# Separate PSUM tiles for the second feed-forward matmul and for the transposes of q and k in a fused retention and feed-forward kernel

## The chip, the cores and the metric

The kernel runs on one core of one Trainium2 chip. The metric is the device time of one execution in microseconds (us). The kernel before takes 328.62 us (median of 3 runs, 328.57 to 328.68). Profiles are of one execution each, and their span is about 2 us shorter than the timed run.

## The reference

Retention with a decay per head, then a feed-forward block with the activation h·cos(h):

```python
# q, k, v: (8 batches, 8 heads, 576 positions, 64), w_in: (512, 2048), w_out: (2048, 512), float32
scores = (1 / np.sqrt(64)) * np.matmul(q, k.transpose(0, 1, 3, 2))
gamma = 1.0 - 2.0 ** (-5.0 - np.arange(H))
Dmat = np.where(rel >= 0, gamma[:, None, None] ** rel[None], 0.0)      # rel = pos_i - pos_j
attn = np.matmul(scores * Dmat, v)
x = attn.transpose(0, 2, 1, 3).reshape(4608, 512)
h = x @ w_in
out = (h * np.cos(h)) @ w_out
```

## The kernel before

The 4608 tokens are handled in 36 groups of 128 (retention) and in 10 chunks (feed-forward) of 512, 256, 256 and then seven times 512 tokens; they are numbered n = 0 to 9 here. A group needs q and k loaded, scaled in bf16 on POOL (`prep`), transposed (on TensorE for groups 0 to 7, by DMA afterwards), and multiplied. A chunk goes through `mm1` (first matmul, sine on ACT, product on DVE) and `mm2` (second matmul in blocks of 128 tokens, each 16 accumulating matmuls of 512 columns, then an eviction by ACT and a DMA out). While `mm2` of one chunk runs, the retention of later groups is slipped in between its matmuls at fixed places.

All PSUM tiles come from one pool with one buffer per tag. Counted in banks, here units of 512 fp32 columns on each partition, the tags a, b and m are two banks wide (an `mm1` block of 1024 fp32 columns), st and n one bank each: the kernel uses eight. A new tile on a tag waits until everything that used the tag's previous tile is done. A write into one part of a tile, in the kernel before, waits for the reader of the tile's other part too, as the trace shows below.

The parts that change:

```python
    def transposes(g, early=False):
        qks, vb, qkT = tiles["a", g]
        # ... groups from 8 on: DMA transpose, and return
        ps = psum.tile([P, 2, 2 * HG, P], BF16, tag="b" if early or g % 2 else "a", name="tr")
        for m in range(2):                                   # m = 0: q, m = 1: k
            for hg in range(HG):
                nc.tensor.transpose(ps[:, m, hg, :],
                    qks[:, m, 2 * hg : 2 * hg + 2, :].rearrange("s h d -> s (h d)"), ident)
            nc.scalar.copy(qkT[:, m * HG : (m + 1) * HG, :], ps[:, m, :HG, :])

    def mm2(n, tsi, et):
        gT = tiles["g", n]
        wide = tsi in (1, 2) if n != 2 else tsi == 0
        if et == 0:
            if not wide:
                tiles["o"] = psum.tile([P, DM], F32, tag="n", name="o")
            elif tsi < 2:
                tiles["oo"] = psum.tile([P, 2, DM], F32, tag="m", name="oo")
        ps = tiles["oo"][:, tsi // 2, :] if wide else tiles["o"]
        nc.tensor.matmul(ps, lhsT=gT[:, et, tsi * P : (tsi + 1) * P],
                         rhs=w_out_sb[:, et, :], start=(et == 0), stop=(et == ET - 1))
        if et == ET - 1:
            ot = op.tile([P, DM], F32, tag="o", name="ot")
            nc.scalar.copy(ot, ps)                           # the eviction
            # ... DMA out, feed(s)

    for g in range(4):                                       # the start
        # ... for g == 3: the weight loads, load(4, gate=w_dma[1]), load(5)
        transposes(g, early=True)
        nc.scalar.copy(tiles["a", g][1], tiles.pop(("fv", g)))
        scores(g, "a")
        if g < 3:
            prep(g + 1, early=True)
        state(g)
        if g < 3:
            attn_out([g], "m")

    # chunk n takes these tags, one per mm1 block:
    banks = {0: "bambambam", 1: "mbam", 2: "bmab", 3: "mamabmab"}.get(n, "bmabmabm")
```

So the four blocks of a 512-token chunk went to n, first half of m, second half of m, n.

## Time and profile before

| quantity | value | view |
|---|---|---|
| time | 328.62 us | timed runs |
| TensorE (PE) busy | 92% | page, part 1 |
| PE in the chain that ended last | 89% | page, part 4 |
| `mm2` waiting for its own eviction | 4.7 us in 7 waits | waits view |
| transposes waiting for ACT's copies | 5.7 us in 8 waits | waits view |

The page of the kernel before, parts 1 and 4 (engine shares):

```profile
PE 299.6 (92%) x2208; PEld 168.8 (52%) x2240; DVE 175.1 (54%) x177; ACT 115.6 (35%) x132; POOL 99.4 (30%) x122
PE 89%; ACT 4%; DVE 2%; issue 2%; DMA 1%; POOL 0%; DVEq 0%; POOLq 0%
```

PE is the bottleneck, so time is won where PE stands still. The waits view says what PE waited for (us in total, times, longest us):

```profile
PE tr L141 <- ACT qkT L146: 5.7, 8, 0.9
PE oo L269 <- ACT ot L278: 4.7, 7, 0.7
PE sc L154 <- ACT qkT L146: 2.7, 4, 0.7
```

The timeline of the last chunk shows one such wait (start us, duration us, engine, line, operation, out<-in, shapes, count, and in brackets the idle time before and its releaser):

```profile
308.31 3.62 PE L269 MATMUL o<-w_out_sb,gT 128*128 128x512 bf16 x16
311.76 3.62 PE L269 MATMUL oo<-w_out_sb,gT 128*128 128x512 bf16 x15
315.41 0.59 ACT L278 COPY ot<-oo 128x512 f32<-128x512 f32 x1 [2.87 <-PE oo L269]
316.05 3.61 PE L269 MATMUL oo<-w_out_sb,gT 128*128 128x512 bf16 x16 [0.67 <-ACT ot L278]
```

A block that is followed without a wait starts 3.45 us before the next one (308.31 to 311.76). The first half of oo starts 4.29 us before the second half. The difference, 0.84 us, is what a wait costs. The profile names only 0.67 us of it, because it counts from the modelled end of the last matmul, which lies about 0.17 us after the point at which the next one could have started. The Trainium skill ("TensorE: Matmul & The Clock Gate", Back-to-back issue gap) gives 512/2.4 + 2.5, about 216 ns, as the gap of a matmul taken by itself; here 3.45 us for 16 in a stream is the same 216 ns each.

A reader who knows the skill's page "Perfetto Trace Analysis" (Optimization Strategy) will recognise the pattern: it says that the same gap repeating on the engine that should be saturated can mean that there isn't enough memory for the next tile, and names buffer count and tile sizes. Here there was enough: the two halves of oo are 512 fp32 each, one bank each. What they shared was the tile.

The timeline at the transposes of groups 4 and 5, inside `mm2` of chunk 0, on PE:

```profile
46.67 0.39 PE L141 MATMUL tr<-ident,qks 128*128 128x128 bf16 x4
47.73 0.38 PE L141 MATMUL tr<-ident,qks 128*128 128x128 bf16 x4 [0.67 <-ACT qkT L146]
49.24 0.39 PE L141 MATMUL tr<-ident,qks 128*128 128x128 bf16 x4
50.57 0.38 PE L141 MATMUL tr<-ident,qks 128*128 128x128 bf16 x4 [0.94 <-ACT qkT L146]
50.79 1.24 PE L269 MATMUL oo<-w_out_sb,gT 128*128 128x512 bf16 x4
```

Four transposes hold PE for 0.22 us (50.57 to 50.79), but k's four start 1.06 us after q's four (46.67 to 47.73), because they write the other half of the tile that ACT is still reading. In groups 6 and 7, in the `mm2` of chunk 1, it is the same:

```profile
67.89 0.38 PE L141 MATMUL tr<-ident,qks 128*128 128x128 bf16 x4 [0.50 <-DVE gT L258]
68.94 0.38 PE L141 MATMUL tr<-ident,qks 128*128 128x128 bf16 x4 [0.67 <-ACT qkT L146]
70.46 0.39 PE L141 MATMUL tr<-ident,qks 128*128 128x128 bf16 x4
71.52 0.38 PE L141 MATMUL tr<-ident,qks 128*128 128x128 bf16 x4 [0.67 <-ACT qkT L146]
```

And the start, where group 3 hands over to the first `mm1` block:

```profile
22.96 0.61 PE L154 MATMUL sc<-qkT 64*128 64x128 bf16 x8 [0.68 <-ACT qkT L146]
23.90 3.62 PE L249 MATMUL h<-xT,w_in_sb 128*128 128x256 bf16 x16
```

### The profile page before, as it was taken

The numbers are of one execution on the slowest core, as the hardware profiler recorded it, in microseconds if no ns is written. First come the engines' busy times: TensorE is split into PE (matmuls) and PEld (weight loads), VectorE is DVE, ScalarE is ACT, GpSimd is POOL, SyncE is SP. The second block draws the span as 40 slices with busy tenths as digits, with TensorE's granted clock in tenths as the row PEclk, the third lists the DMA queues.
The fourth block names the chain that finished last, engine by engine and source line by source line (L and its number), as shares of the span: only waits on it lengthen the run. The fifth ranks groups of instructions, "written<-read, shape, count | busy, mean of one in ns | idle before, by whom it ended". The sixth has DMA issues, their size and how long they took to land.

```text
span 326.7 us, 5413 instructions
## 1 busy us (share of the span) xinstructions
PE 299.6 (92%) x2208; PEld 168.8 (52%) x2240; DVE 175.1 (54%) x177; ACT 115.6 (35%) x132; POOL 99.4 (30%) x122
## 2 busy tenths in 40 slices
PE   1669998979999989998999899989998999899995
PEld 1447844746768745444544454445444544454442
DVE  2644624345686755475547554765476546654600
ACT  4253632351515510551065105510551056105611
POOL 3670066662363635430633053305430000000000
PEclk9999999999999999999999999999999999999999
DMA  9999999999999999955992599259932610010011
GB/s 171 214 156 195 213 228 245 218 230 177 167 225 217 235 227 256 184 91 130 245 227 44 127 241 236 42 121 241 228 57 65 115 49 0 34 64 34 0 64 64
DMA packets 151512, 49.63 MB, mean 152 GB/s; under 512 B 142784, under 2 KB 146880, under 8 KB 151488
## 3 DMA queue, kind: packets, MB, share of 16 engines
q1 hardware_dynamic: 147264, 45.10, 72.9%
q0 software_dynamic: 4224, 4.19, 8.0%
q8 instruction: 17, 0.28, 0.4%
q14 instruction: 7, 0.06, 0.1%
HBM read 36.70 MB, written 9.44 MB: 141 GB/s over the span
## 4 chain that ended last, share of the span: by engine, by line
PE 89%; ACT 4%; DVE 2%; issue 2%; DMA 1%; POOL 0%; DVEq 0%; POOLq 0%
PE h L249 38%; PE oo L269 20%; PE o L269 19%; PE sc L154 3%; PE ov L224 3%; PE st L182 2%; ACT qkT L146 2%; PE tr L141 2%; PE ov L211 2%; ACT ot L278 2%; DVE ret L163 2%; DMA fq<-in_q_dram 1%; ACT cosh L257 1%; DVE gT L258 0%; POOL qks L124 0%
## 5 line engine op out<-in xcount | busy, mean ns | idle before, releaser
L249 PE MATMUL h<-xT,w_in_sb 128*128 128x256 bf16 (+1 forms) x762 | 128.6, 329 | 0.6 <-DVE ret L163 0.2
L258 DVE TENSOR_TENSOR gT<-h,cosh 128x1024 bf16<-128x1024 f32 x72 | 88.2, 1225 | 64.2 <-ACT cosh L257 64.0
L249 PEld LDWEIGHTS <-w_in_sb 128*128 128x128 bf16 x768 | 75.8, 99 | 51.9 <-issue 1.0
L257 ACT ACTIVATE cosh<-h,half_pi 128x1024 f32<-128x1024 f32 x72 | 80.2, 1113 | 54.8 <-PE h L249 54.8
L269 PEld LDWEIGHTS <-gT 128*128 128x128 bf16 x576 | 52.4, 98 | 62.2 <-issue 6.7
L124 POOL TENSOR_TENSOR qks<-fq,gq 128x512 bf16<-128x512 f32 x36 | 37.5, 1042 | 127.9 <-DMA fq<-in_q_dram 120.4
L269 PE MATMUL oo<-w_out_sb,gT 128*128 128x512 bf16 x278 | 68.5, 379 | 5.7 <-ACT ot L278 4.7
L269 PE MATMUL o<-w_out_sb,gT 128*128 128x512 bf16 x272 | 67.6, 379 | 1.6 <-issue 1.1
L163 DVE TENSOR_TENSOR ret<-sc,tri 128x1024 bf16<-128x1024 f32 x32 | 38.0, 1220 | 18.0 <-PE sc L154 18.0
L125 POOL TENSOR_TENSOR qks<-fk,gk 128x512 bf16<-128x512 f32 x34 | 35.4, 1042 | 6.7 <-DMA fk<-in_k_dram 5.2
L236 DVE CAST xT<-ov 128x1024 bf16<-128x1024 f32 (+1 forms) x20 | 22.3, 1116 | 25.7 <-PE ov L224 25.4
L278 ACT COPY ot<-oo 128x512 f32<-128x512 f32 x18 | 10.5, 586 | 71.1 <-PE oo L269 66.3
L191 DVE TENSOR_TENSOR sb<-st,diag_99 128x512 bf16<-128x512 f32 x32 | 21.9, 683 | 22.1 <-PE st L182 22.1
L278 ACT COPY ot<-o 128x512 f32<-128x512 f32 x18 | 10.5, 585 | 62.7 <-PE o L269 62.7
L131 POOL CAST vb<-fv 128x512 bf16<-128x512 f32 x32 | 19.5, 610 | 5.3 <-DMA fv<-in_v_dram 3.9
L141 PE MATMUL tr<-ident,qks 128*128 128x128 bf16 x64 | 7.8, 261 | 11.4 <-ACT qkT L146 5.7
L146 ACT COPY qkT<-tr 128x512 bf16<-128x512 bf16 x16 | 9.4, 586 | 18.6 <-PE tr L141 18.6
L154 PE MATMUL sc<-qkT 64*128 64x128 bf16 x288 | 12.4, 227 | 2.7 <-ACT qkT L146 2.7
L224 PE MATMUL ov<-ret,vb 128*64 128x128 bf16 x288 | 12.8, 232 | 1.6 <-DVE ret L163 1.6
L154 PEld LDWEIGHTS <-qkT 64*128 64x128 bf16 x288 | 8.5, 98 | 10.6 <-issue 5.9
L182 PEld LDWEIGHTS <-qks 128*128 128x128 bf16 (+1 forms) x128 | 9.6, 102 | 7.8 <-issue 2.5
L182 PE MATMUL st<-vb,qks 128*128 128x128 bf16 (+1 forms) x128 | 13.3, 230 | 0.0
(31 smaller groups left out, 56.0 us busy)
## 6 DMA issues: line engine op xcount, KB each, us to landing
out_dram<-ot SPq DMA_DIRECT2D x36, 256.0 KB, 3.7
fq<-in_q_dram SPq DMA_DIRECT2D x32, 256.0 KB, 4.3
fk<-in_k_dram SPq DMA_DIRECT2D x32, 256.0 KB, 4.7
fv<-in_v_dram SPq DMA_DIRECT2D x32, 256.0 KB, 4.8
w_in_sb<-in_moe_w_in_dram POOLq DMA_DIRECT2D x4, 512.0 KB, 8.5
w_out_sb<-in_moe_w_out_dram POOLq DMA_DIRECT2D x4, 512.0 KB, 16.3
fq<-in_q_dram SPq DMA_DIRECT2D x8, 128.0 KB, 4.8
fk<-in_k_dram SPq DMA_DIRECT2D x8, 128.0 KB, 5.1
```

Of the source, the lines that this page charges most:

```text
L124: nc.gpsimd.tensor_tensor(out=qks[:, 0], in0=fq, in1=tq, op=ALU.mult)
L125: (nc.vector if early and g in (0, 3) else nc.gpsimd).tensor_tensor(out=qks[:, 1], in0=fk, in1=tk, op=ALU.mult)
L154: nc.tensor.matmul(ps[:, he, hg, :], lhsT=qkT[d0 : d0 + D, HG + hg, :], rhs=qkT[d0 : d0 + D, hg, :], start=True, stop=True,)
L163: nc.vector.tensor_tensor(out=ret.rearrange("p a b i -> p (a b) i"), in0=ps.rearrange("p a b i -> p (a b) i"), in1=mask.unsqueeze(1).to_br ...
L182: nc.tensor.matmul(ps[:, hg, :], lhsT=qks[p0:, 1, 2 * hg : 2 * hg + 2, :].rearrange("s h d -> s (h d)"), rhs=vb[p0:, 2 * hg : 2 * hg + 2, ...
L224: nc.tensor.matmul(ps[he * D : he * D + D, x, hg, :], lhsT=vb[:, 2 * hg + he, :], rhs=ret[:, he, hg, :], start=(g % PER == 0 and hg == 0), ...
L236: nc.vector.tensor_copy(tiles["x", n][:, :, t0 : t0 + len(gs) * P].rearrange("p c (x i) -> p x c i", i=P), ps)
L249: nc.tensor.matmul(ps[:, j, :], lhsT=w_in_sb[:, dg, (et + j) * P : (et + j + 1) * P], rhs=xT[:, dg, c0 : c0 + w], start=(dg == 0), stop=(d ...
L257: nc.scalar.activation(cosh, ps, ACTF.Sin, bias=half_pi, scale=1.0)
L258: nc.vector.tensor_mul(gT[:, et : et + m, c0 : c0 + w], ps, cosh)
L269: nc.tensor.matmul(ps, lhsT=gT[:, et, tsi * P : (tsi + 1) * P], rhs=w_out_sb[:, et, :], start=(et == 0), stop=(et == ET - 1),)
L278: nc.scalar.copy(ot, ps)
```

## The change

The intent is to take these waits away without another bank: `mm2` alternates over two separate tiles (n, m, n, m), q and k are transposed into a tile each, and in the first four groups the q transpose of the next group goes ahead of the output matmuls of this one. No instruction is added or removed.

```diff
-    def transposes(g, early=False):
+    def transposes(g, banks=None, only=(0, 1)):
@@
-        ps = psum.tile([P, 2, 2 * HG, P], BF16, tag="b" if early or g % 2 else "a", name="tr")
-        for m in range(2):
+        for m in only:
+            ps = psum.tile([P, HG, P], BF16, tag=banks[m], name="tr")
             for hg in range(HG):
                 nc.tensor.transpose(
-                    ps[:, m, hg, :],
+                    ps[:, hg, :],
@@
-            nc.scalar.copy(qkT[:, m * HG : (m + 1) * HG, :], ps[:, m, :HG, :])
+            nc.scalar.copy(qkT[:, m * HG : (m + 1) * HG, :], ps)
@@ mm2
-        wide = tsi in (1, 2) if n != 2 else tsi == 0
         if et == 0:
-            if not wide:
-                tiles["o"] = psum.tile([P, DM], F32, tag="n", name="o")
-            elif tsi < 2:
-                tiles["oo"] = psum.tile([P, 2, DM], F32, tag="m", name="oo")
-        ps = tiles["oo"][:, tsi // 2, :] if wide else tiles["o"]
+            bank = "mn"[tsi % 2] if n == 2 else "nm"[tsi % 2]
+            tiles["o"] = psum.tile([P, DM], F32, tag=bank, name="o")
+        ps = tiles["o"]
@@ the start
-        transposes(g, early=True)
+        if g == 0:
+            transposes(g, "bn", only=(0,))
+        transposes(g, "bn", only=(1,))
@@
         if g < 3:
+            transposes(g + 1, "bn", only=(0,))
             attn_out([g], "m")
@@ groups 4 to 7
-        return [(place, lambda: transposes(g)), (place + 6, lambda: transposes(g + 1))]
+        return [
+            (place, lambda: transposes(g, "ab")),
+            (place + 6, lambda: transposes(g + 1, "ab")),
+        ]
```

## The prediction

> **What bounds the kernel now.** TensorE. The page gives PE 92% busy, the chain of waits is 89% PE, and the granted clock stays at 9 tenths or more. Idle time of PE in that chain can be won; the waits view names it: the second matmul's tile "oo" waits for its eviction by ACT 7 times (4.7 us of modelled idle time), transposes wait for ACT's copies 8 times (5.7 us).
>
> **What the change does.** No instruction is added or removed; only tiles and order change.
>
> 1. *Second matmul, chunks of 512 tokens (n = 3 to 9).* Before, blocks 1 and 2 are two halves of one tile, and block 2 starts only after block 1's eviction. In the last chunk (timeline) block 1 starts at 311.76 us and block 2 at 316.05, 4.29 us later. The Trainium skill ("TensorE: Matmul & The Clock Gate", Back-to-back issue gap) gives 512/2.4 + 2.5 = about 216 ns per matmul; the trace agrees: 308.31 to 311.76 is 16 matmuls, 216 ns each. So block 2 could start at 315.2, and the wait costs 0.84 us (ACT copy 0.59, the rest pipeline drain). With alternating tiles the order is n, m, n, m: each tile has 3.5 us to be evicted. Seven times 0.84 = 5.9 us off.
>
> 2. *A new wait.* Block 3 of the first chunk now lies in m, and the second chunk's first matmul block also takes m: it waits one eviction, +0.84 us. Later chunks start with another tile (or, after the 256-wide chunk, end on n), and their m block comes at least 8 matmuls (1.7 us) later: no wait.
>
> 3. *Transposes of groups 6 and 7.* q and k halves no longer wait for each other: today the transposes of k start 1.05 us after those of q, though four take 0.22. Two times 0.83 = 1.7 us off.
>
> 4. *Start (groups 0 to 3) and groups 4, 5.* Today a group takes 5.05 us. With the q transposes ahead, about 1.25 us leaves each turn; then loads and POOL's scaling (q1 ready at 8.7, q2 at 12.3, q3 at 15.9) begin to matter. I expect the scores of group 3 at about 19 us instead of 22.96. But the first h matmul needs the first part of w_in: issued at 15.86, fastest landing 5.6 us, so about 21.5 to 22 instead of 23.9. About 2 us gained. The transposes of groups 4 and 5 then lose their waits too (0.83 and 1.1 us), but k of group 5 leaves POOL at 48.2 us whatever PE does (DMA-bound). So the mm2 stream resumes at 48.5 instead of 50.79: 2.3 us gained in all up to there, rather than 4.
>
> **Sum:** -5.9 + 0.84 - 1.7 - 2.3 = -9.1 us, nearly all on the critical path, as PE is the chain. Predicted 319.6 us (2.8% faster), 8 in 10 between 318.2 and 321.3. Faster by over 2%: 0.92; within 2%: 0.07; slower: 0.01.
>
> **What would show it.** Waits of the second matmul for the ot copy vanish; one new wait of h for ot near 58 us, about 0.7 us; transposes of group 5 wait for POOL about 1 us; h starts at 21.5 to 22, waiting for the w_in DMA; each chunk from n = 3 on is 0.84 us shorter.
>
> **What would make it wrong.** Earlier work collides on the DMA queues (over 90% busy until 139 us) and delays group 5 or the weights; weights land later than I read; a PE clock that warms earlier or later at the start.

## The result

The changed kernel takes 319.69 us (median of 4 runs, 319.60 to 319.76), against 328.65 us before in the same rounds. The ratio is 0.9727 (95% interval 0.971 to 0.9744): 2.7% faster. Ratios here are the mean time of one kernel's runs over that of the other's of the same rounds, so not quite the ratio of the medians that are quoted.

The page of the changed kernel, parts 1 and 4:

```profile
PE 297.4 (94%) x2208; PEld 167.5 (53%) x2240; DVE 175.2 (55%) x177; ACT 115.6 (36%) x132; POOL 99.7 (31%) x122
PE 81%; DMA 8%; SPq 5%; POOL 2%; issue 2%; DVE 1%; ACT 1%
```

PE is still the bottleneck, but the chain has a new beginning: until 48 us it now runs through DMA, the load queue (SPq) and POOL. Its longest piece is the landing of a part of w_out (19.89 to 34.60 us), which the loads of groups 4 and 5 are made to wait for (`gate`); no run moved this gate. What stands in the waits view for PE, of the waits that matter here:

```profile
PE sc L154 <- ACT qkT L146: 2.7, 4, 0.7
PE h L249 <- DMA w_in_sb<-in_moe_w_in_dram: 1.5, 1, 1.5
PE tr L141 <- POOL qks L125: 0.8, 1, 0.8
PE h L249 <- ACT ot L275: 0.7, 1, 0.7
```

The waits of `mm2` for its eviction and of the transposes for ACT are gone; one wait of h for the eviction is new. The last chunk is one unbroken stream, from the timeline:

```profile
299.99 13.98 PE L266 MATMUL o<-w_out_sb,gT 128*128 128x512 bf16 x63
```

The transposes of groups 4 and 5, the first `mm1` block of chunk 1, and the transposes of groups 6 and 7, on PE:

```profile
44.02 0.72 PE L141 MATMUL tr<-ident,qks 128*128 128x128 bf16 x8
44.58 1.46 PE L266 MATMUL o<-w_out_sb,gT 128*128 128x512 bf16 x6
46.89 0.40 PE L141 MATMUL tr<-ident,qks 128*128 128x128 bf16 x4 [0.86 <-POOL qks L124]
48.07 0.40 PE L141 MATMUL tr<-ident,qks 128*128 128x128 bf16 x4 [0.78 <-POOL qks L125]
48.30 1.24 PE L266 MATMUL o<-w_out_sb,gT 128*128 128x512 bf16 x4
...
58.38 7.15 PE L249 MATMUL h<-xT,w_in_sb 128*128 128x256 bf16 x64 [0.67 <-ACT ot L275]
66.24 0.61 PE L141 MATMUL tr<-ident,qks 128*128 128x128 bf16 x8 [0.72 <-DVE gT L258]
...
67.98 0.61 PE L141 MATMUL tr<-ident,qks 128*128 128x128 bf16 x8
```

The eight transposes of groups 4, 6 and 7 now run as one piece each. Group 5's no longer wait for ACT, but for POOL, which scales that group's q and k almost back to back:

```profile
45.79 1.04 POOL L124 TENSOR_TENSOR qks<-fq,gq 128x512 bf16<-128x512 f32 x1 [0.35 <-DMA fq<-in_q_dram]
46.97 1.04 POOL L125 TENSOR_TENSOR qks<-fk,gk 128x512 bf16<-128x512 f32 x1
```

And the start:

```profile
19.14 0.40 PE L154 MATMUL sc<-qkT 64*128 64x128 bf16 x8 [0.68 <-ACT qkT L146]
21.58 3.12 PE L249 MATMUL h<-xT,w_in_sb 128*128 128x256 bf16 x16 [1.54 <-DMA w_in_sb<-in_moe_w_in_dram]
```

The scores of group 3 come 3.8 us earlier, the first h only 2.3 us earlier: it waits for the first part of w_in.

Where the time went can be followed by laying the same event of both timelines side by side. The last column is the growth of the lead from row to row. Single profiles scatter: in the seven profiles here of kernels that transpose these groups in separate tiles and leave the loads as they were, `mm2` resumes between 48.20 and 48.55 us.

| event (start on PE) | before, us | after, us | lead, us | growth |
|---|---|---|---|---|
| first h of chunk 0 | 23.90 | 21.58 | 2.32 | 2.32 |
| `mm2` resumes after group 5's transposes | 50.79 | 48.30 | 2.49 | 0.17 |
| first h of chunk 1 | 60.02 | 58.38 | 1.64 | -0.85 |
| first h of chunk 2 | 79.44 | 76.13 | 3.31 | 1.67 |
| first h of chunk 3 | 96.00 | 92.68 | 3.32 | 0.01 |
| first h of chunk 4 | 130.84 | 126.68 | 4.16 | 0.84 |
| first h of chunk 5 | 163.30 | 158.32 | 4.98 | 0.82 |
| first h of chunk 6 | 196.32 | 190.50 | 5.82 | 0.84 |
| first h of chunk 7 | 228.78 | 222.13 | 6.65 | 0.83 |
| first h of chunk 8 | 261.80 | 254.32 | 7.48 | 0.83 |
| first h of chunk 9 | 294.49 | 286.17 | 8.32 | 0.84 |
| end of the span | 326.7 | 317.5 | 9.2 | 0.9 |

### The profile page after: what moved, and what is told of

Read it like the earlier page. It is cut to its first block, busy times and chain, and to the rows that moved or that the text cites. A ratio compares the mean times of both kernels' runs of the same rounds, so it can differ in the third digit from the quotient of the medians.

```text
span 317.5 us, 5415 instructions
## 1 busy us (share of the span) xinstructions
PE 297.4 (94%) x2208; PEld 167.5 (53%) x2240; DVE 175.2 (55%) x177; ACT 115.6 (36%) x132; POOL 99.7 (31%) x122
## 4 chain that ended last, share of the span: by engine, by line
PE 81%; DMA 8%; SPq 5%; POOL 2%; issue 2%; DVE 1%; ACT 1%
PE o L266 37%; PE h L249 34%; SPq L101 5%; DMA w_out_sb<-in_moe_w_out_dram 5%; PE ov L224 3%; PE sc L154 3%; PE st L182 2%; PE ov L211 2%; DMA fk<-in_k_dram 2%; DMA fq<-in_q_dram 2%; POOL w_in_sb L328 1%; PE tr L141 0%; DVE ret L163 0%; DVE gT L258 0%; ACT ot L275 0%
## 5 line engine op out<-in xcount | busy, mean ns | idle before, releaser
L266 PE MATMUL o<-w_out_sb,gT 128*128 128x512 bf16 x550 | 132.7, 379 | 2.5 <-issue 1.8
L275 ACT COPY ot<-o 128x512 f32<-128x512 f32 x36 | 21.1, 586 | 127.7 <-PE o L266 123.5
L211 PEld LDWEIGHTS <-sb 128*128 128x128 bf16 x128 | 8.9, 103 | 3.7
L141 PEld LDWEIGHTS <-qks 128*128 128x128 bf16 x64 | 4.9, 115 | 10.9 <-POOL qks L124 7.3
```

## The experiments

Four kernels ran on the first chip (before: 328.27 us), four on the second (before: 328.64 us), four on the third (before: 328.33 us). The same kernel's median moved by up to 0.4 us from chip to chip, so terms below a microsecond are read from the traces. The 95% intervals of the ratios are at most 0.0017 to either side (0.0025 for the transposes alone). With its threshold of 2%, the record calls the two halves "same" and the kernel with groups 4 to 7 shared "unclear"; all three are nevertheless faster than before by more than the noise. All twelve gave correct results.

### Only the second matmul's tiles

```diff
 (the kernel before, with only this)
-        wide = tsi in (1, 2) if n != 2 else tsi == 0
-        ... tiles "o" on n and "oo" on m
+        bank = "mn"[tsi % 2] if n == 2 else "nm"[tsi % 2]
+        tiles["o"] = psum.tile([P, DM], F32, tag=bank, name="o")
```

> The kernel before with only the second matmul's alternation over two tiles. If the terms of the prediction are additive: 7 waits of 0.84 us go, one new wait of 0.84 us comes before the first h block of the second chunk, so 328.65 - 5.9 + 0.84 = about 323.6 us; the second matmul's stream after the transposes of group 5 resumes at 50.8 us as before. Rival: the start of the kernel carries most of the gain and the tiles of the second matmul little: then above 326 us.

Measured: 323.75 us (323.62 to 323.89), ratio 0.9861. The span fell from 326.7 to 321.5 us, 5.2 us, where 5.06 was expected. `mm2` resumed after the transposes at 50.65 us, as before, and h of chunk 1 waited 0.67 us for the eviction. The rival, that the tiles matter little, falls.

### Only the transposes

```diff
 (the changed kernel, with the second matmul's tiles put back)
-        bank = "mn"[tsi % 2] if n == 2 else "nm"[tsi % 2]
-        tiles["o"] = psum.tile([P, DM], F32, tag=bank, name="o")
+        wide = tsi in (1, 2) if n != 2 else tsi == 0
+        ... tiles "o" on n and "oo" on m
```

> The changed kernel with the second matmul put back on its old tiles. Additive: only the start (2.5 us by 48.3 us) and the transposes of groups 6 and 7 (1.7 us) are gained, so 328.65 - 4.2 = about 324.5 us, the seven waits of the oo matmuls for the eviction are back, and the wait of h for the eviction near 58 us is gone. Together with the run of the other half the two gains should add up to the whole change's 9.0 us within 0.3. Rival: the halves interact, and the sum differs by over 1 us.

Measured: 324.51 us (three runs within 0.10 us, one at 326.04), ratio 0.9894. The span is 322.5 us, 4.2 us less than before, as expected. The waits view has the seven waits back, and no wait of h for the eviction:

```profile
PE oo L269 <- ACT ot L278: 4.7, 7, 0.7
```

The two halves save 5.2 and 4.2 us of span, 9.4 together; the whole change saves 9.2. Read from these single profiles, they add up within 0.3 us, as expected. The medians don't resolve this: the halves save 4.5 and 3.8 us, 8.3 together, against 9.0 for the whole change in its own rounds and 8.3 in its repetition on the third chip (below). So no interaction shows that the scatter, some 0.7 us between these figures, would let one see.

### Without the q transpose ahead

```diff
-        if g == 0:
-            transposes(g, "bn", only=(0,))
-        transposes(g, "bn", only=(1,))
+        transposes(g, "bn")
@@
-            transposes(g + 1, "bn", only=(0,))
```

> The changed kernel without the q transpose ahead in groups 0 to 3 (the separate bank tiles stay). Theory: moving q ahead is off the critical path, because h then waits for w_in until about 21.6 us and the stream after group 5's transposes for POOL until 48.3 us. The scores of group 3 should come at about 20.4 us instead of 19.1, h still at 21.6, the time 319.7 us within 0.3. Rival: the groups' chain at the start sets the time, and about 1.2 us is lost: 320.9 us.

Measured: 319.98 us (319.82 to 320.26), ratio 0.9746. That was 0.3 us above the changed kernel, but on another chip, so both ran again:

> The changed kernel once more, as the reference on the same chip for the three runs that follow: 319.7 us within 0.3.

> The kernel without the q transpose ahead, once more, since the first try (319.98 us) left open whether 0.3 us is real. Theory (off the critical path): within 0.2 us of the changed kernel of this call. Rival (a small part lies on the path): 0.3 us or more slower in every round.

Measured: the changed kernel 320.04 us (319.57 to 320.17, ratio 0.9748), without q ahead 319.82 us (319.71 to 320.21, ratio 0.9744). There is no difference that the scatter would let one see. The trace of the first try shows why, on PE:

```profile
20.17 0.61 PE L154 MATMUL sc<-qkT 64*128 64x128 bf16 x8 [0.74 <-ACT qkT L146]
...
21.51 3.60 PE L249 MATMUL h<-xT,w_in_sb 128*128 128x256 bf16 x16 [0.20 <-DMA w_in_sb<-in_moe_w_in_dram]
...
48.45 1.24 PE L266 MATMUL o<-w_out_sb,gT 128*128 128x512 bf16 x4
```

The scores of group 3 are 1.0 us later than with q ahead, and it costs nothing: h starts at the same time, because it waits for w_in, only shorter (0.20 instead of 1.54 us). The part of the change that reorders instructions is off the critical path, though not by much: in this kernel the groups finish only 0.2 us before w_in lands. The separate tiles alone bring a group down from 5.05 to 4.27 us (scores at 11.62, 15.89 and 20.17), moving q ahead to about 3.9. What the start as a whole is worth can be read from two other runs: the kernel with only the second matmul's tiles and the one with groups 4 to 7 shared (below) differ in the start alone. `mm2` resumes at 50.65 and 48.69 us there, and the spans are 321.5 and 319.6 us: about 1.9 us.

The repetition of the changed kernel also shows a caution about the waits view. In it PE's transposes of group 5 are put down to ACT (0.66 us for "ACT ot"), while the weight load just ahead of them is put down to POOL; POOL ended that scaling at 46.88 us, ACT its copy at 46.90 us, and the transposes began at 46.94 us. Two releasers ended within 0.02 us, and the view names the later one.

### The first chunk starts on m

```diff
-            bank = "mn"[tsi % 2] if n == 2 else "nm"[tsi % 2]
+            bank = "mn"[tsi % 2] if n in (0, 2) else "nm"[tsi % 2]
```

> The changed kernel with the first chunk's second matmul starting on tile m and ending on n, so that the second chunk's first h block finds m free. Theory: the new wait costs one eviction[...], so 0.84 us is gained: 318.85 us, and the wait of h for the eviction copy near 58 us is gone. Rival: the h block would then wait for something else at that place (its input xT), and little is gained: within 0.3 us of 319.7.

Measured: 318.96 us (318.80 to 319.08), ratio 0.9714. The new wait is gone from the trace:

```profile
48.55 1.24 PE L266 MATMUL o<-w_out_sb,gT 128*128 128x512 bf16 x4
...
57.78 4.42 PE L249 MATMUL h<-xT,w_in_sb 128*128 128x256 bf16 x39
```

From the resumption to h it takes 9.23 us (57.78 - 48.55), against 10.08 us in the changed kernel (58.38 - 48.30): 0.85 us less. This letter in one string is a small mistake in the change, and its repair costs nothing.

### q and k loads of groups 4 and 5 ahead of their v loads

```diff
-            load(4, gate=w_dma[1])
-            load(5)
+            load(4, gate=w_dma[1], names="qk")
+            load(5, names="qk")
+            load(4, names="v")
+            load(5, names="v")
@@ (and the scalings on POOL in the same order)
```

> The changed kernel with the q and k loads (and their scaling) of groups 4 and 5 ahead of the v loads of both. Theory: the second matmul's stream stops before the transposes of group 5 because k of group 5 lands at about 46.9 us; one 256 KB load earlier in the queue is about 1.2 us, so the stream resumes at about 47.1 instead of 48.3 and the time is about 318.5 us (318.0 to 319.0). The waits of the transposes for POOL shrink from 1.6 us to about 0.8 or less. Rival: another thing (copies on ACT, v of group 4) takes the place of that wait, and the time stays within 0.3 us of 319.7.

Measured: 319.35 us (318.43 to 319.46), ratio 0.9715. The time missed the expected range (318.0 to 319.0). `mm2` resumed at 47.85 us, earlier than 48.30 but not at 47.1. In this execution POOL did the four scalings from 43.02 to 47.56 us, without a wait for a load from 44.52 us on. PE itself reached the transposes of group 5 only at 47.14 us and then waited 0.2 us for POOL. The gate of these loads, a landed part of w_out, also fell 0.8 us later than in the changed kernel's profile (the loads began at 35.41 instead of 34.62 us), and `mm2` had a wait of 0.35 us for w_out. Which of these delays counted most was not separated. Seen alone on its chip, 0.3 us could not be told from the scatter.

### Groups 4 to 7 in a shared tile again

```diff
-            (place, lambda: transposes(g, "ab")),
-            (place + 6, lambda: transposes(g + 1, "ab")),
+            (place, lambda: transposes_shared(g)),        # the old form: one tile, two halves
+            (place + 6, lambda: transposes_shared(g + 1)),
```

> The changed kernel with q and k of groups 4 to 7 transposed into one shared tile again, as before. Theory: groups 6 and 7 lose 0.83 us each; for groups 4 and 5 the lost time lies under the wait for POOL at 48 us and costs nothing: 319.7 + 1.7 = about 321.4 us, resumption still at 48.3 to 48.6 us. Rival: all four cost 0.83 us: 323.0 us.

Measured: 321.73 us (321.50 to 321.93), ratio 0.9793. `mm2` resumed at 48.69 us, 0.4 us later than in the changed kernel's profile, and in groups 6 and 7 k's transposes again started 1.05 us after q's, where 0.22 would do: 2 x 0.83 us. Together 2.1 us, which is the difference of the spans (319.6 and 317.5 us). Group 5, on PE:

```profile
47.39 0.40 PE L153 MATMUL tr<-ident,qks 128*128 128x128 bf16 x4
48.46 0.39 PE L153 MATMUL tr<-ident,qks 128*128 128x128 bf16 x4 [0.67 <-ACT qkT L158]
48.69 1.24 PE L278 MATMUL o<-w_out_sb,gT 128*128 128x512 bf16 x5
```

So of the four waits, the two of groups 4 and 5 cost 0.4 us together and not 1.7 (0.1 to 0.5 us, given the scatter of the resumption): they lie mostly under the wait for POOL. The rival, 323.0 us, falls.

### Every block on one tile

```diff
-            bank = "mn"[tsi % 2] if n == 2 else "nm"[tsi % 2]
+            bank = "n"
```

> The changed kernel with every block of the second matmul on the one tile n, so that each block waits for the eviction of the one before it. Theory: 0.84 us for each of three boundaries in seven chunks of 512 tokens (17.6 us), one to two more in the first chunk and one in each 256-wide chunk, less the wait of h for m, which goes; a few hidden tenths where state matmuls lie at the boundary: about 337 us (335 to 339). Rival: the waits partly hide behind each other or behind the attention work, and the cost is under 12 us.

Measured: 337.62 us (337.25 to 338.01), ratio 1.0277. That is 17.9 us more than the changed kernel. The waits view and the last chunk:

```profile
PE o L266 <- ACT ot L275: 15.6, 25, 0.7
...
319.71 3.61 PE L266 MATMUL o<-w_out_sb,gT 128*128 128x512 bf16 x16 [0.67 <-ACT ot L275]
324.00 3.61 PE L266 MATMUL o<-w_out_sb,gT 128*128 128x512 bf16 x16 [0.67 <-ACT ot L275]
328.28 3.61 PE L266 MATMUL o<-w_out_sb,gT 128*128 128x512 bf16 x16 [0.67 <-ACT ot L275]
```

(The first line is from the waits view, the others from the timeline.) The blocks are 4.28 and 4.29 us apart instead of 3.45. The 25 waits are three in each of the seven 512-token chunks, two in the first chunk and one in each 256-wide chunk. From the first h of one chunk to that of the next, a 512-token chunk now takes 2.1 to 2.5 us more than in the changed kernel, a 256-wide chunk 0.84 us more; the first chunk costs nothing net, since the new wait of h went. So the price of one boundary is 0.84 us where nothing else fills it; at the third boundary of most chunks retention work fills a part (the wait named there is 0.35 to 0.45 us).

### Both repairs together, and k of group 5 on DVE

The first kernel joins the tile order of the first chunk and the load order. The second adds, at place 31 of chunk 0's `mm2`:

```diff
-        nc.gpsimd.tensor_tensor(out=qks[:, 1], in0=fk, in1=tk, op=ALU.mult)       # group 5, POOL
+        nc.vector.tensor_tensor(out=qks[:, 1], in0=fk, in1=tk, op=ALU.mult)       # group 5, DVE
```

> The changed kernel with both repairs: the first chunk's second matmul starting on m, and the q and k loads of groups 4 and 5 ahead of their v loads. If the two waits are independent the gains add: 319.7 - 0.84 - 1.2 = about 317.6 us (317.0 to 318.2). Rival: the earlier stream only runs into the next wait (m not free, v of group 4 late), and one of the gains is lost: above 318.3 us.

> Both repairs once more, beside the changed kernel on the same chip: 0.84 us for the first chunk's tile order and 0.5 to 0.7 us for the load order (the trace of the first try showed the stream resuming at 47.6 instead of 48.3 us): 1.3 to 1.5 us faster than the changed kernel of this call.

> Both repairs, and k of group 5 scaled on DVE (0.69 us) instead of POOL (1.04 us). If the landing of k of group 5 at about 46.2 us and its scaling are what holds the stream, it resumes 0.3 us earlier, at about 47.3 us, and the time is 0.3 us below that of both repairs. Rival: DVE gets to it late, or the transposes then wait for ACT: no gain.

Measured: both repairs 318.39 us (317.94 to 319.37), ratio 0.9695, and 318.51 us (317.91 to 318.76), ratio 0.9699. On the third chip (the second of these two) that is 1.5 us less than the changed kernel beside it (320.04 us), as the second expectation had it; the first expectation, 317.6 us, was too good by 0.8 us, and the measured 318.39 us fell where its rival had been put (above 318.3). The part that came short is the load order: `mm2` resumed at 47.60 us in the first and 47.39 in the second, 0.7 and 0.9 us earlier than in the changed kernel's 48.30 and not 1.2. Here, other than with the load order alone, POOL stood waiting for k of group 5 to land (from the timeline of the first):

```profile
46.27 1.04 POOL L127 TENSOR_TENSOR qks<-fk,gk 128x512 bf16<-128x512 f32 x1 [0.63 <-DMA fk<-in_k_dram]
```

With k of group 5 on DVE: 317.78 us (317.74 to 318.08), ratio 0.9682, 0.7 us less than both repairs by the medians, but the ranges of the two overlap, and the traces show `mm2` resuming at 47.39 and 47.37 us, where 0.3 us between them was expected. The median moved the way the theory said; that the scaling on DVE is what moved it is not shown. DVE began the scaling as soon as k had landed:

```profile
46.39 0.69 DVE L128 TENSOR_TENSOR qks<-fk,gk 128x512 bf16<-128x512 f32 x1 [5.00 <-DMA fk<-in_k_dram]
```

The landing of k of group 5 is then what its scaling waits for, as it was with both repairs. This last version has the lowest median of all: 3.2% below the kernel before.

## Why the prediction was right

The prediction said 319.6 us (318.2 to 321.3), and 319.69 us was measured. Each term of its sum held:

- **Seven waits of the second matmul, 5.9 us.** Held. From chunk 3 on the lead grows by 0.82 to 0.84 us per 512-token chunk. The half of the change alone (5.2 us of span) and the kernel with one tile (17.9 us for 25 waits, some of them partly filled) show that it is the reuse of the tile that costs this.
- **A new wait of 0.84 us ahead of chunk 1.** Held: the lead falls by 0.85 us there, and giving the tile order of the first chunk the other letter wins 0.85 us back.
- **Transposes of groups 6 and 7, 1.7 us.** Held: the lead grows by 1.67 us, and the shared tile brings back 2 x 0.83 us.
- **The start and groups 4 and 5, 2.3 us.** Held, at 2.49 us in these two profiles. The scores of group 3 came at 19.14 us (19 was said), h at 21.58 (21.5 to 22), `mm2` resumed at 48.30 (48.5). The important half of this step was to stop adding: PE saves 3.8 us up to group 3's scores, of which h keeps 2.3 because w_in lands at 21.5 us, and what the transposes of groups 4 and 5 lose in waits is taken up by the wait for POOL. That wait also levels what lies between: chunk 0's `mm2` began 2.83 us earlier (38.23 against 41.06), and 2.49 us were left after it.
- **The reason given for that wait was half right.** The prediction calls k of group 5 "DMA-bound". In the changed kernel's profile q of group 5 waits for its load (0.35 us), and then POOL scales q and k almost back to back (45.79 and 46.97 us, 1.04 us each). It is load and POOL together, and moving the loads forward alone brought 0.45 us at the resumption of the expected 1.2 us. The transposes of group 5 waited 0.86 and 0.78 us for POOL, 1.6 us in all, where the prediction said about 1.
- **What the prediction did not say:** the q transpose ahead, a third of the change by its description, is worth nothing here. It follows from the prediction's own numbers (scores at 19 us, w_in at 21.5), and the kernel without it shows it. The prediction also put the whole 1.25 us that leaves each group down to q going ahead; about 0.8 of it comes from the separate tiles (5.05 to 4.27 us). The sum was safe from this slip because w_in, and then load and POOL, set the time up to there.

## What to carry to other kernels

In this kernel a PSUM tile with two halves was one tile to the waits: the second half's first matmul waited until the first half was evicted, though each half is a bank of its own. Measure one such wait by how much farther apart the starts of successive blocks lie (4.29 instead of 3.45 us, so 0.84 us), not by the idle time that the profile names (0.67 us), and count the boundaries that nothing fills. When alternating over tiles that other phases use too, check who takes each tile next: the order in one chunk decided whether 0.84 us was lost. And before adding up gains at the start, look for the first thing that PE cannot hasten (weights landing, loads and scaling of the next groups): gains ahead of it count only up to there.

## What the Trainium skill lacked or had wrong

- "TensorE: Matmul & The Clock Gate", Back-to-back issue gap: it says that a stream of weight load and matmul pairs sustains about 131 ns per matmul of 512 columns, and that the formula 512/2.4 + 2.5 over-counts there. Here a stream of exactly such pairs runs at 216 ns each (16 in 3.45 us, before and after), so the formula holds and the lower figure does not appear.
- The same page, PE-mode transpose, gives about 275 ns for a transpose in a kernel's context. The durations in this trace are like that (216 to 314 ns), but four in a row hold PE for only 0.22 us at a granted clock of 1.00 (50.57 to 50.79 us before): 55 ns each. That section lacks the rate of a series, which is what counts here; the formula above comes to 55.8 ns for 128 columns, which fits.
- "Perfetto Trace Analysis", Optimization Strategy, gives too little memory for the next tile (buffer count, tile sizes) as a possible reason of a repeating gap. It doesn't name the one that made the seven gaps of 0.84 us here: two blocks in one tile while a second tile stood free. The same eight banks, divided otherwise, removed them.
- No page looked at gives the price of reusing a PSUM tile at once: 0.84 us from the missed start of a 512-column matmul to the real one, with ACT's copy of 128x512 fp32 (0.59 us) in between.
